# Attention stage of a fused attention and mixture-of-experts kernel: a cap on how far scores run ahead, gate products by head pair, two banks for the last outputs

## The chip, the cores and the metric

The kernel runs on one core of a Trainium2 chip. The metric is the device time of one execution in microseconds (us); lower is better. A program in the kernel file writes out the instructions of every engine in a fixed order, and each engine works through its own list in that order.

## What is computed

Four batches of eight heads, 768 tokens, head width 64, go through a local attention with block summaries; the result is the input of two mixture-of-experts layers (8 experts, 512 to 1024 to 512).

```python
k_sum = k.reshape(B, H, nb, block, D).max(axis=3)      # 24 blocks of 32 keys
v_sum = v.reshape(B, H, nb, block, D).mean(axis=3)
scores = concat(masked scale*q@k.T (|i-j| < 16), scale*q@k_sum.T + log(32))
a = softmax(scores);  attn = a @ concat(v, v_sum)
x = attn.transpose(0, 2, 1, 3).reshape(3072, 512)
logits = x @ w_gate + modality_bias[modality_id];  e = argmax(logits)
x = gate_weight * (relu(x @ w1[e]) @ w2[e])            # first expert layer
x = second expert layer: each expert takes the 384 tokens assigned to it by greedy capacity
```

## The kernel before, in words

The change lies in the attention stage and in the program that orders it. The work of the stage is cut into 48 **groups** (`QUADS`): four batches, four head pairs (`HP`), three groups per head pair. Group i has 256 query rows of two heads, and these steps:

- `scores` (L318, step "s"): eight matmuls of 64 rows into a PSUM bank with tag "s" (two such banks).
- `top_` (L330, "m"): VectorE takes the row maxima and scales them. `expo` (L335, "e"): ScalarE does four exponentials.
- `atrans` (L341, "at"): four transposes on TensorE into a bank "a" (two). `atput` (L347, "ac"): ScalarE or VectorE copies them to SBUF.
- `av` (L351, "av"): eight matmuls with the values, into the bank "o"; there is one.
- `total`, `inverse`, `put_x` (L363 to L378, "t", "r", "x"): VectorE divides by the row sums and puts the result into `xb`, which also frees the bank "o".
- `xturn` (L425, "xt"): two transposes of the result into a bank "t" (two). `xput` (L433, "xp"): a copy to SBUF, tile `xt`, three buffers.
- `gate1` (L437, "g1"): two matmuls with 8 weight columns each, which add the group's part of the gate logits in the bank `GS`. At the end of a batch come `gcopy`, `gturn`, `gput` (L449 to L461, "gc", "gt", "gp") and the batch's routing (`route1`, L505).

Once three batches are routed, `first_page` (L698) lists the first 256 tokens of the most frequent expert, gathers their rows through GpSimd's DMA queue (`gather`, L643) and issues the first four quarter loads of the expert weights (`wraw`) on SyncE's queue. `first_turn` and `first_split` ("ft", "fs") transpose and split these rows, `Quarters.high` and `low` ("hi", "lo") split the first four weight quarters into a high and a low part, all among the last groups of the attention.

**What sets the order.** `Pieces` (L753) holds every step with an order number, the engines that may take it, the steps it must follow, and the buffers it needs. `step` (L780) works with a cost model (`Clock`, L67): at each turn it takes the step that can start earliest by the model, and among those that can start then the one with the lowest order number. The step's instructions are written out at that moment, so an engine's list follows the model's times, while the chip keeps its own. The order numbers count groups: scores of group i have i, products with values i + 3, gate steps i + 5 (`LOG`), and i + 10 (`LOGT`) for the last eight groups. The rules that bound how far scores run ahead are indirect: scores of group i follow the exponentials of group i - 2, these follow the transposes of group i - 4 and so on. `av(i)` follows `put_x(i - 1)`, because there is one bank "o". The loop ends (L893) when every step is written out; the code of the first expert layer comes behind it, so on TensorE its first matmul (`s<-xhi,whi`) stands behind the last step of the attention.

Of the kernel before, what the change touches and what calls it, by code (L numbers as in the profile page):

```python
# [8 lines left out]
F32 = mybir.dt.float32  # L9
# [14 lines left out]
HP = H // 2  # L24
E = 8
# [13 lines left out]
QUADS = B * HP * 3  # L39
# [101 lines left out]
def moe_block(ctx, tc, qt, kw, vw, v, mod, wg1, mbias, w1a, w2a, wg2, w1b, w2b, out):  # L141
# [138 lines left out]
    def vsum(i):  # L280
# [9 lines left out]
        else:  # L290
            VB[0] = vb

    XB = {}
    PS, NM, EX, AT, RD = {}, {}, {}, {}, {}

# [54 lines left out]

    def av(i):  # L351
        g, c = divmod(i, 3)
        p = bank("o")
        PS["o", i] = pv = p[:, :4 * (D + 1)].rearrange("p (u c) -> p u c", u=4)
        for t in range(2):
            for h in range(2):
                for s in range(2):
                    P.matmul(pv[s * 64:(s + 1) * 64, 2 * t + h, :],
                             AT[i][:UC, 2 * t + h, s * 64:(s + 1) * 64],
                             VW[g % NV][:UC, s, h, 2 * c + t, :], start=True, stop=True)  # L360
        AT.pop(i)
# [59 lines left out]
    XS = {}  # L421
# [9 lines left out]
            P.transpose(p[:, t * 128:(t + 1) * 128], XB[b][:, 2 * c + t, hp * 128:(hp + 1) * 128], ident)  # L431

    def xput(j, e):  # L433
        XS[j] = ld.tile([128, 256], F32, name="xt", bufs=3)
        copy(e, XS[j], PS.pop(("x", j))[:, :256])

    def gate1(j):  # L437

        g, c = divmod(j, 3)
        b, hp = divmod(g, HP)  # L440
        x, o = XS.pop(j), (b % 2) * 256 + c // 2 * 128
        if hp == c == 0:
            P.matmul(GS[0][:, o:o + 256], zb, zb[:, None, :].to_broadcast([128, 2, 128]), start=True, stop=False, skip_group_check=True)
        for t in range(2):
            r0 = 32 * (2 * (c % 2) + t)
            P.matmul(GS[0][r0:r0 + E, o:o + 128], wg1s[:, hp], x[:, t * 128:(t + 1) * 128], start=False, stop=(hp == HP - 1),
                     skip_group_check=True)

    def gcopy(b, e):  # L449
        XS["g", b] = t = ld.tile([128, 256], F32, name="gst", bufs=1)  # L450
# [278 lines left out]
    EPA = 0  # L729
    GRP = -3.5  # L730
    AHEAD = 4
    LOGT = 10
    HL = 1000
    LOG = 5
    THR = -10
    BIAS = 0.3
    WARM = 6
# [15 lines left out]
    class Pieces:  # L753
# [26 lines left out]
        def step(self):  # L780
            best = {}
            for name, (order, on, fn, after, take, give, cost) in self.todo.items():
                if any(x not in self.end for x in after) or take and not self.free():
                    continue
                t, e = min((self.start(e, after, take) + (BIAS if len(on) > 1 and e == "V" else 0.0), e) for e in on)
                best.setdefault(e, []).append((t, order, name))
            if self.thread is None and self.queue and self.queue[0][1] in self.end:
                self.thread, self.want, self.ready = self.queue.pop(0)[0], "V", 0.0
            if self.thread and (self.want != "P" or self.free()):
                e = "P" if self.want == "P" else "V"  # L790
                best.setdefault(e, []).append((max(clock.at[e], self.ready), THR + self.base, None))
            lo = {e: min(x) for e, x in best.items()}
            e = min(lo, key=lambda x: lo[x])
            t = lo[e][0]
            name = min((x for x in best[e] if x[0] <= t + EPA), key=lambda x: x[1])[2]
            clock.last = 0.0
            if name is None:
                if self.want == "P":
                    self.slots.append([("thread",), None])
                was, self.want = self.want, next(self.thread, None)  # L800
                if was != "P":
                    self.give(("thread",))
                self.ready = clock.after("P" if self.want == "P" else "V")
                if self.want is None:
                    self.thread = None
                return
            order, on, fn, after, take, give, cost = self.todo.pop(name)
            self.base = order if name[0] == "s" else self.base
            if take:
                self.slots.append([name, None])  # L810
            for x in after:
                if e in "VAP" and x[0] in ("lk", "lq", "lv", "lvs", "lvb", "fv", "fi", "qs", "c"):
                    clock.at[e] = max(clock.at[e], self.end[x])
            if cost is not None:
                clock.at[e] = clock.last = max(clock.at[e], t) + cost
            if len(on) > 1:
                fn(e)
            else:
                fn()
            if give:  # L820
                self.give(give)
            self.end[name], self.by[name] = clock.last + (2.0 if e == "D" else 0.0), e
# [7 lines left out]
    for g in range(NG):  # L830
# [12 lines left out]
        for c in range(3):  # L843
            i = 3 * g + c
            pc.add(("s", i), i, "P", L_(scores, i),
                   [("kc", h, g) for h in range(2)] + [("lq", g)]
                   + [("s", i - 1), ("e", i - 2)])
            pc.add(("m", i), i + OM, "V", L_(top_, i), [("s", i), ("e", i - 3), ("m", i - 1)])
            pc.add(("e", i), i + OE, "A", L_(expo, i), [("m", i), ("e", i - 1), ("at", i - 4)])
            pc.add(("at", i), i + OAT, "P", L_(atrans, i), [("e", i), ("ac", i - 2), ("at", i - 1)])  # L850
            pc.add(("ac", i), i + OAC, "AV", L_(atput, i), [("at", i), ("ac", i - 1), ("av", i - 3)])
            pc.add(("av", i), i + OAV, "P", L_(av, i), [("ac", i), ("av", i - 1), ("x", i - 1), ("lv", g), ("vr", g)])
            pc.add(("t", i), i + OX, "V", L_(total, i), [("av", i)])
            pc.add(("r", i), i + OX, "V", L_(inverse, i), [("t", i)])
            old = 3 * HP * (b - 1) - 1
            pc.add(("x", i), i + OX, "V", L_(put_x, i), [("r", i), ("x", i - 1)] + ([("xt", old), ("sx", old)] if b > 1 else []))
            if g % HP == HP - 1:
                pc.add(("sx", i), i, "D", L_(store_x, b, c), [("x", i)], cost=1.5)
            pc.add(("xt", i), i + (LOG if i < QUADS - 8 else LOGT), "P", L_(xturn, i), [("x", i), ("xt", i - 1)], take=1)
            pc.add(("xp", i), i + OXP + (LOG if i < QUADS - 8 else LOGT), "AV", L_(xput, i), [("xt", i), ("xp", i - 1), ("g1", i - 3)], give=("xt", i))  # L860
            pc.add(("g1", i), i + (LOG if i < QUADS - 8 else LOGT), "P", L_(gate1, i), [("xp", i), ("g1", i - 1), ("lc", 0)])
        if g % HP == HP - 1:
            o = 3 * g + 2 + (LOG if g < NG - 3 else LOGT)
            pc.add(("gc", b), o + OGP, "AV", L_(gcopy, b), [("g1", 3 * g + 2)])
            pc.add(("gt", b), o + OGP, "P", L_(gturn, b), [("gc", b)], take=1)
            pc.add(("gp", b), o + OGP, "V", L_(gput, b), [("gt", b), ("bc", 0)], give=("gt", b))
    zl = qk.tile([128, NTOK // 128 * E], F32, name="zl")
# [1014 lines left out]
```

## Time and profile before

| | us |
|---|---|
| median of three runs (885.65 to 888.65) | 886.11 |
| the profiled execution: its time | 885.47 |
| its span, first to last instruction | 883.6 |
| TensorE busy (share of the span) | 800.4 (91%) |
| VectorE busy | 669.1 (76%) |
| ScalarE busy | 423.9 (48%) |
| mean granted TensorE clock | 0.958 |

In the profile, "line" is L136 for nearly everything, since one helper issues the compute instructions; the tile names tell the steps apart: `s<-kw,qt` scores, `a<-ident,ex` the transposes behind the exponentials, `o<-vw,at` products with values, `t<-ident,xb` the transposes of results, `gs<-xt,wg1s` gate products, `t<-ident,xr` the transposes of the first gathered rows, `s<-xhi,whi` the first expert matmul. An fp32 matmul leaves two records: a group has 16 records of scores, 16 of products, 4 of gate products; a transpose leaves one. A timeline row gives start and length of a run of like instructions; the next run can start before the end of the one before it, since matmuls overlap. PEclk 1.00 is 2.4 GHz and 0.50 is 1.2 GHz.

### The profile page before, as it was taken

How to read it: one execution, taken by the hardware profiler on the slowest of the kernel's cores; microseconds unless marked ns; L12 is line 12 of the kernel's file. 1: busy time of each engine (PE TensorE's matmuls, PEld its weight loads, DVE VectorE, ACT ScalarE, POOL GpSimd, SP SyncE). 2: the span in 40 equal slices, each digit the busy share in tenths (PEclk: the TensorE clock that was granted, in tenths of full speed). 3: DMA queues.
4: the chain of work that ended last, by engine and by line, in shares of the span. 5: the costliest groups of instructions: out<-in, count | busy, mean ns of one | idle time of the engine just before them, and what ended most of it. 6: DMA issues, size and time to landing. Idle time of an engine off the chain costs nothing. (4 is left out here: it accounts for less than half of the span.)

```text
span 883.6 us, 17809 instructions
## 1 busy us (share of the span) xinstructions
PE 800.4 (91%) x6457; PEld 672.1 (76%) x6457; DVE 669.1 (76%) x1908; ACT 423.9 (48%) x769; POOL 223.7 (25%) x354
## 2 busy tenths in 40 slices
PE   4888899779999999999999924999999999998997
PEld 3666667558998899999999822878786878787895
DVE  7978786659884888888888758788797979786540
ACT  4665566443566855555555512334343343333440
POOL 6453821302142233223322212011112020204011
PEclk9999989879999999999999955999999999999999
DMA  7789866455679576656665304253434353437410
GB/s 243 226 255 314 269 214 198 148 168 167 212 245 329 170 239 224 208 200 216 227 200 198 119 22 143 84 178 104 160 112 163 120 167 120 145 119 245 143 65 36
DMA packets 93093, 157.16 MB, mean 178 GB/s; under 512 B 10332, under 2 KB 53620, under 8 KB 92228
## 3 DMA queue, kind: packets, MB, share of 16 engines
q1 hardware_dynamic: 83652, 128.91, 45.6%
q0 software_dynamic: 8800, 25.96, 8.6%
q8 instruction: 53, 0.87, 0.4%
q10 hardware_dynamic: 544, 1.05, 0.4%
q14 instruction: 44, 0.36, 0.1%
HBM read 136.36 MB, written 19.53 MB: 176 GB/s over the span
## 5 line engine op out<-in xcount | busy, mean ns | idle before, releaser
L136 DVE TENSOR_TENSOR wlo<-wraw,whi 128x512 fp32r<-128x512 f32 x336 | 218.6, 685 | 21.9 <-ACT whi L136 20.3
L136 ACT ACTIVATE whi<-wraw 128x1024 fp32r<-128x1024 f32 x168 | 176.2, 1056 | 61.0 <-DMA wraw<-in_moe_w_dram 59.4
L136 PE MATMUL s<-xhi,whi 128*128 128x256 f32 (+1 forms) x640 | 197.4, 311 | 2.2 <-DVE hlo L136 1.5
L136 PE MATMUL s<-xhi,wlo 128*128 128x256 f32 (+1 forms) x640 | 196.2, 309 | 0.0
L136 PE MATMUL s<-xlo,whi 128*128 128x256 f32 (+1 forms) x640 | 189.3, 310 | 0.0
L136 PE MATMUL a<-wlo,hhi 128*128 128x512 f32 x328 | 131.4, 401 | 0.0
L136 PE MATMUL a<-whi,hhi 128*128 128x512 f32 x328 | 130.1, 397 | 0.0
L136 PE MATMUL a<-whi,hlo 128*128 128x512 f32 x328 | 129.5, 395 | 0.0
L136 PEld LDWEIGHTS s<-xhi,whi 128*128 128x128 f32 x640 | 122.6, 191 | 5.6 <-ACT xhi L136 3.0
L136 PEld LDWEIGHTS s<-xhi,wlo 128*128 128x128 f32 x640 | 122.6, 192 | 0.7
L136 ACT ACTIVATE hhi<-s 128x384 fp32r<-128x384 f32 (+1 forms) x112 | 60.0, 535 | 130.6 <-PE s L136 130.5
L136 PEld LDWEIGHTS s<-xlo,whi 128*128 128x128 f32 x640 | 119.6, 191 | 0.2
L136 DVE SCALAR_TENSOR_TENSOR hlo<-s,hhi 128x384 fp32r<-128x384 f32 (+1 forms) x112 | 68.0, 608 | 22.3 <-ACT hhi L136 22.1
L136 PEld LDWEIGHTS a<-whi,hlo 128*128 128x128 f32 x328 | 61.7, 188 | 11.9
L136 PEld LDWEIGHTS a<-whi,hhi 128*128 128x128 f32 x328 | 61.7, 188 | 11.9
L136 PEld LDWEIGHTS a<-wlo,hhi 128*128 128x128 f32 x328 | 61.7, 188 | 11.1
L136 ACT ACTIVATE ex<-s,nm 128x120 f32<-128x120 f32 x192 | 53.6, 365 | 32.8 <-DVE nm L136 28.7
L1763 POOL DMA_INDIRECT xr<-y_d,ix x24 | 26.5, 1105 | 165.5 <-DVE key L136 123.4
L136 PE MATMUL s<-kw,qt 128*64 128x120 f32 x768 | 54.6, 289 | 11.3 <-ACT kw L136 9.7
L136 ACT ACTIVATE xhi<-t 128x512 fp32r<-128x512 f32 x49 | 28.1, 596 | 73.5 <-PE t L136 73.5
L1094 POOL DMA_INDIRECT y_d<-y,six x25 | 30.5, 1219 | 112.6 <-ACT y L136 109.8
L136 PEld LDWEIGHTS s<-kw,qt 128*64 128x64 f32 x768 | 42.9, 147 | 20.9 <-ACT kw L136 11.0
(305 smaller groups left out, 1258.2 us busy)
## 6 DMA issues: line engine op xcount, KB each, us to landing
wraw<-in_moe_w_dram SPq DMA_DIRECT2D x166, 512.0 KB
kw<-in_kw_dram SPq DMA_DIRECT2D x32, 324.0 KB
vw<-in_vw_dram SPq DMA_DIRECT2D x32, 292.5 KB
vb<-in_v_dram SPq DMA_DIRECT2D x6, 1024.0 KB
qt<-in_qt_dram SPq DMA_DIRECT2D x32, 192.0 KB
x_d<-xb SPq DMA_DIRECT2D x12, 512.0 KB
hr<-in_moe_w_gate_dram SPq DMA_DIRECT2D x4, 512.0 KB
wraw<-in_moe_w_dram ACTq DMA_DIRECT2D x2, 512.0 KB
```

The costliest lines, as they stand in the source:

```text
L136: return fn(*args, **kw)
L1094: st = G.indirect_dma_start(out=dst, out_offset=bass.IndirectOffsetOnAxis(ap=six[:, c:c + 1], axis=0), in_=rows, in_offset=None)
L1763: G.indirect_dma_start(out=t, out_offset=None, in_=y_d[:NTOK], in_offset=bass.IndirectOffsetOnAxis(ap=IX[k][:, i:i + 1], axis=0))
```

## The change

1. **Cap on scores.** Scores of group i must also follow the products of group i - 4 (`LAG = 4`).
2. **Two banks at the end.** The products of groups 45 and 47 (`SPARE`) go to a bank with tag "s". Products of groups 45 to 47 follow `put_x` of the group two back, not one back.
3. **Gate products by head pair.** `gate1` is called once per head pair, behind the three `xput` of its groups, and issues the six matmuls in one run. `xt` has four buffers.
4. **Order numbers of the gate steps**: i + 4 everywhere (`LOG = 4`); `LOGT` is gone.
5. **Planner's start times**: for "hi" and "ft" the model now counts when the weight quarter or the gathered rows land (`clock.ready`).

```diff
+    SPARE = (QUADS - 3, QUADS - 1)
...
     def av(i):
         g, c = divmod(i, 3)
-        p = bank("o")
+        p = bank("s" if i in SPARE else "o")
...
-        XS[j] = ld.tile([128, 256], F32, name="xt", bufs=3)
+        XS[j] = ld.tile([128, 256], F32, name="xt", bufs=4)
...
-    def gate1(j):
-
-        g, c = divmod(j, 3)
+    def gate1(g):
+
         b, hp = divmod(g, HP)
-        x, o = XS.pop(j), (b % 2) * 256 + c // 2 * 128
-        if hp == c == 0:
+        o = b % 2 * 256
+        if hp == 0:
             P.matmul(GS[0][:, o:o + 256], zb, zb[:, None, :].to_broadcast([128, 2, 128]), start=True, stop=False, skip_group_check=True)
-        for t in range(2):
-            r0 = 32 * (2 * (c % 2) + t)
-            P.matmul(GS[0][r0:r0 + E, o:o + 128], wg1s[:, hp], x[:, t * 128:(t + 1) * 128], start=False, stop=(hp == HP - 1),
-                     skip_group_check=True)
+        for c in range(3):
+            x = XS.pop(3 * g + c)
+            for t in range(2):
+                r0, o1 = 32 * (2 * (c % 2) + t), o + c // 2 * 128
+                P.matmul(GS[0][r0:r0 + E, o1:o1 + 128], wg1s[:, hp], x[:, t * 128:(t + 1) * 128], start=False, stop=(hp == HP - 1),
+                         skip_group_check=True)
...
-    LOGT = 10
-    LOG = 5
+    LOG = 4
+    LAG = 4
...
+                x = QS[0].raw.get(name[1]) if name[0] == "hi" else XR.get(name[1]) if name[0] == "ft" else None
+                if x is not None:
+                    t = max(t, clock.ready(x, e))
...
             pc.add(("s", i), i, "P", L_(scores, i),
                    [("kc", h, g) for h in range(2)] + [("lq", g)]
-                   + [("s", i - 1), ("e", i - 2)])
+                   + [("s", i - 1), ("e", i - 2), ("av", i - LAG)])
...
-            pc.add(("av", i), i + OAV, "P", L_(av, i), [("ac", i), ("av", i - 1), ("x", i - 1), ("lv", g), ("vr", g)])
+            pc.add(("av", i), i + OAV, "P", L_(av, i), [("ac", i), ("av", i - 1), ("x", i - (2 if i in SPARE or i - 1 in SPARE else 1)), ("lv", g), ("vr", g)])
...
-            pc.add(("xp", i), i + OXP + (LOG if i < QUADS - 8 else LOGT), "AV", L_(xput, i), [("xt", i), ("xp", i - 1), ("g1", i - 3)], give=("xt", i))
-            pc.add(("g1", i), i + (LOG if i < QUADS - 8 else LOGT), "P", L_(gate1, i), [("xp", i), ("g1", i - 1), ("lc", 0)])
+            pc.add(("xp", i), i + OXP + LOG, "AV", L_(xput, i), [("xt", i), ("xp", i - 1), ("g1", (i - 4) // 3)], give=("xt", i))
+        pc.add(("g1", g), 3 * g + 2 + LOG, "P", L_(gate1, g), [("xp", 3 * g + c) for c in range(3)] + [("g1", g - 1), ("lc", 0)])
```

## Rows read from the trace of the kernel before

**Rows 1.** Page, part 2: granted TensorE clock in 40 slices of the span (tenths).
```profile
PEclk9999989879999999999999955999999999999999
```
**Rows 2.** Busy time of each engine by stretch, in us; last columns clock, DMA share, GB/s.
```profile
core 0: us, PE busy (x) PEld busy (x) DVE busy (x) ACT busy (x) POOL busy (x), PEclk, DMA share, GB/s
...
171.22:178.09 6.87, 6.87 (x57) 5.04 (x57) 3.38 (x10) 3.29 (x6) 2.69 (x11) 0.56 0.08 30
...
183.99:192.28 8.29, 6.21 (x53) 3.42 (x53) 1.53 (x6) 1.65 (x5) 0.00 (x0) 0.50 0.86 282
13.72:163.88 150.16, 133.73 (x1862) 102.07 (x1862) 117.92 (x328) 91.70 (x285) 63.20 (x114) 0.95 0.77 240
...
192.28:883.60 691.32, 643.89 (x4371) 556.01 (x4369) 524.97 (x1510) 314.05 (x451) 144.50 (x198) 0.97 0.50 162
```
**Rows 3.** The same view for tile qt: the PE count is score records, 16 a group.
```profile
27.60:50.70 23.10, 9.16 (x128) 7.18 (x128) 0.00 (x0) 0.00 (x0) 0.00 (x0) 0.94 0.77 242
...
85.10:102.20 17.10, 6.25 (x96) 4.88 (x96) 0.00 (x0) 0.00 (x0) 0.00 (x0) 1.00 0.72 242
...
0.00:50.70 50.70, 16.78 (x208) 13.32 (x208) 1.62 (x1) 1.65 (x2) 3.31 (x3) 0.97 0.79 244
0.00:102.20 102.20, 33.60 (x464) 26.58 (x464) 1.62 (x1) 1.65 (x2) 3.31 (x3) 0.97 0.82 254
0.00:131.40 131.40, 44.18 (x608) 34.81 (x608) 1.62 (x1) 1.65 (x2) 3.31 (x3) 0.95 0.81 255
0.00:163.87 163.87, 53.55 (x752) 42.13 (x752) 1.62 (x1) 1.65 (x2) 3.31 (x3) 0.96 0.76 237
```
**Rows 4.** The same for tile vw (PE, PEld, POOL): product records, 16 a group.
```profile
163.87:192.28 28.41, 6.69 (x112) 5.59 (x112) 0.00 (x0) 0.73 0.67 214
...
0.00:50.70 50.70, 6.64 (x144) 5.72 (x144) 6.41 (x18) 0.97 0.79 244
0.00:102.20 102.20, 17.26 (x368) 14.60 (x368) 19.72 (x46) 0.97 0.82 254
0.00:131.40 131.40, 22.87 (x480) 19.52 (x480) 24.33 (x56) 0.95 0.81 255
0.00:163.87 163.87, 30.47 (x656) 25.85 (x656) 31.18 (x70) 0.96 0.76 237
```
**Rows 5.** Timeline of TensorE, 135 to 143 us: start, length, what.
```profile
135.20 0.69 PE L136 MATMUL o<-vw,at 120*64 120x65 f32 x16
135.82 0.44 PE L136 MATMUL t<-ident,xb 128*128 128x128 f32 x2
136.18 1.04 PE L136 MATMUL s<-kw,qt 128*64 128x120 f32 x16
137.16 0.39 PE L136 MATMUL gs<-xt,wg1s 128*8 128x128 f32 x4
137.48 0.69 PE L136 MATMUL o<-vw,at 120*64 120x65 f32 x16
...
141.86 1.04 PE L136 MATMUL s<-kw,qt 128*64 128x120 f32 x16
142.73 0.46 PE L136 MATMUL o<-vw,at 120*64 120x65 f32 x10
```
**Rows 6.** Timeline of TensorE, 162 to 193 us; in brackets idle before and releaser.
```profile
162.90 0.69 PE L136 MATMUL o<-vw,at 120*64 120x65 f32 x16 [1.68 <-DVE mk L136]
...
171.22 1.09 PE L136 MATMUL t<-ident,xr 128*128 128x128 f32 x4 [3.78 <-DMA xr<-x_d,gix]
...
178.09 0.61 PE L136 MATMUL gs<-xt,wg1s 128*8 128x128 f32 x8
178.63 0.69 PE L136 MATMUL o<-vw,at 120*64 120x65 f32 x16
...
186.81 1.14 PE L136 MATMUL o<-vw,at 120*64 120x65 f32 x16
...
192.28 0.56 PE L136 MATMUL s<-xhi,whi 128*128 128x256 f32 x1
```
**Rows 7.** Timeline of ScalarE, 163 to 192 us.
```profile
166.03 1.12 ACT L136 ACTIVATE ex<-s,nm 128x120 f32<-128x120 f32 x4 [0.46 <-DVE nm L136]
...
179.64 0.59 ACT L136 ACTIVATE at<-a 120x512 f32<-120x512 f32 x1
```
**Rows 8.** Timeline of SyncE's queue, 150 to 206 us.
```profile
161.65 2.12 SPq L589 DMA_DIRECT2D wraw<-in_moe_w_dram  x4
177.57 6.22 SPq L592 DMA_DIRECT2D wraw<-in_moe_w_dram  x4
```

More of the change, by code (lines that the diff above doesn't have):

```diff
@@ L858, in moe_block @@
                 pc.add(("sx", i), i, "D", L_(store_x, b, c), [("x", i)], cost=1.5)
-            pc.add(("xt", i), i + (LOG if i < QUADS - 8 else LOGT), "P", L_(xturn, i), [("x", i), ("xt", i - 1)], take=1)
-            pc.add(("xp", i), i + OXP + (LOG if i < QUADS - 8 else LOGT), "AV", L_(xput, i), [("xt", i), ("xp", i - 1), ("g1", i - 3)], give=("xt", i))
-            pc.add(("g1", i), i + (LOG if i < QUADS - 8 else LOGT), "P", L_(gate1, i), [("xp", i), ("g1", i - 1), ("lc", 0)])
+            pc.add(("xt", i), i + LOG, "P", L_(xturn, i), [("x", i), ("xt", i - 1)], take=1)
+            pc.add(("xp", i), i + OXP + LOG, "AV", L_(xput, i), [("xt", i), ("xp", i - 1), ("g1", (i - 4) // 3)], give=("xt", i))
+        pc.add(("g1", g), 3 * g + 2 + LOG, "P", L_(gate1, g), [("xp", 3 * g + c) for c in range(3)] + [("g1", g - 1), ("lc", 0)])
         if g % HP == HP - 1:
-            o = 3 * g + 2 + (LOG if g < NG - 3 else LOGT)
-            pc.add(("gc", b), o + OGP, "AV", L_(gcopy, b), [("g1", 3 * g + 2)])
+            o = 3 * g + 2 + LOG
+            pc.add(("gc", b), o + OGP, "AV", L_(gcopy, b), [("g1", g)])
             pc.add(("gt", b), o + OGP, "P", L_(gturn, b), [("gc", b)], take=1)
```

## The prediction

> **What bounds the kernel now.** I read the page's clock line first [rows 1]: of 40 slices of 22 us two are at half, and the rest near full. The dip near 540 us lies in the second routing, which the change does not touch. For the attention I went from the clock to busy time by stretch [rows 2]. From 13.72 to 163.88 us TensorE is busy 133.73 of 150.16 us (89%), VectorE 117.92 (79%), ScalarE 91.70 (61%): TensorE sets the pace with some holes. From 183.99 to 192.28 us its clock is 0.50 and it is still idle for 2.08 of 8.29 us, with VectorE and ScalarE at a fifth: nothing is the bound there but a chain of single steps.
>
> The counts by tile say why that tail is long. At 163.87 us 752/16 = 47 groups of scores have run [rows 3], but only 656/16 = 41 groups of products [rows 4]. Behind it come one group of scores and 112/16 = 7 groups of products [rows 4], in 28.4 us. In the timeline [rows 6] that stretch holds a wait of 3.78 us for the first gathered rows, whose transposes stand in TensorE's list ahead of products that could have run; the clock is 0.56 in the 6.87 us behind it [rows 2]. Then the products come one at a time through the single bank "o", each with its transposes and a gate product that waits for a copy, until the first expert matmul at 192.28 us.
>
> **The change part by part.** I follow one number, the start of the first expert matmul; what lies behind it takes 691.32 us [rows 2].
>
> *Last scores, moved products.* With the cap four products are left behind the last scores instead of seven, so three run ahead of them. One costs TensorE 0.62 us for the products (135.20 to 135.82), 0.36 for the transposes (135.82 to 136.18) and 0.32 for the gate (137.16 to 137.48) [rows 5]: 1.30, so the last scores move by +3.9 us. They started at 163.88 us.
>
> *Gate products.* A pair costs 0.32 us. Eight records, two pairs in one run, cost 178.63 - 178.09 = 0.54 [rows 6], so a further pair costs 0.22 and a run of three 0.76 instead of 0.96. The pair also costs the group ahead of it: scores take 0.98 us to the start of a gate pair but 0.87 to the start of products [rows 5], 0.11 more, twice saved per run. In all 0.20 + 0.22 = 0.42 us per head pair, 6.3 us over the 15 runs ahead of the last scores. This counts where TensorE is the bound. Bounds: 0 (a wait takes it) and -6.3; TensorE is busy 89%, but VectorE's 79% is near, so I take -3.7, somewhat over half.
>
> *What the cap takes away.* The lead of scores over products was 13 - 9 = 4 at 50.70 us, 29 - 23 = 6 at 102.20, 38 - 30 = 8 at 131.40 and 47 - 41 = 6 at 163.87 [rows 3, 4]. It rose by about five groups in all, counting the part ahead of 50.70 as one. Where it rose, scores filled time in which products were late; now TensorE waits there. The price of a lost fill is at most the scores and the transposes behind them, 0.98 + 0.6 = 1.6 us, so 8 us in all; at the least nothing, where the planner merely preferred scores to products that were ready. A small gain is not excluded either. That work isn't gone: it is done later, in place of the scores that ran ahead before, and the count of work ahead of the last scores is the same but for the three products above. I take +4: the place at 162.90 us, where products waited 1.68 us for VectorE's routing burst [rows 6] although the lead was 6, says that late products are real. Queued behind such a wait are the next scores, and VectorE's maxima wait for them.
>
> *The planner's start times.* With the landing counted, the gathered rows' transposes no longer stand ahead of ready products: the 3.78 us wait goes, and so does the cold stretch behind it. The next thing late is the chain of the last group. The weight splits move the same way on ScalarE and VectorE; they lie beside the chain and can each delay one of its steps by up to an instruction. GpSimd's two gathers and SyncE's first four quarter loads (161.65 us [rows 8]) hang on the gate of the third batch, which comes somewhat earlier.
>
> *The last chain.* From the last scores at 163.88 to the end of their exponentials at 166.03 + 1.12 = 167.15 us are 3.27 us [rows 7]. Then four transposes (at most 0.7, twice the pair's 0.36), their copy 0.59 [rows 7] and two handovers, about 0.1 each: 4.8 us to the last products. The three products that are left before it fit into this time, 3 x 1.30 = 3.9, since two more banks hold them: this is what hides them. With one bank each would wait for the division of the one before. From the last products at 186.81 to the expert matmul at 192.28 are 5.47 us [rows 6], at half clock. The last run of gate products is now three pairs, 0.76 for 0.32: +0.4. In all 10.7 us, which I take; at full clock the second half shortens, by about 1.3 us (products 0.69 for 1.14, the rest in like proportion).
>
> On the clock in this chain: the trace shows 0.50 in 183.99 to 192.28, where TensorE worked in short runs with waits between [rows 2]. The Trainium skill, "TensorE: Matmul & The Clock Gate", section on a second failure mode (depth-cycling of the PSUM queue), says that short idles between groups that cycle through banks can make the clock swing between its two levels. It speaks against this change, which leaves a tail of just this kind and may add waits in the middle; by it the chain is 10.7 us as taken, and at full clock it would be 9.4.
>
> On the gate run: the trace shows pairs in one pair of column positions only. The Trainium skill, "TensorEngine Tiling (Array Packing)", Key Properties, says that different tiles can load and multiply in parallel; by that the first four products of a run would go together and a run would cost 0.54, not 0.76, another 3.3 us over 15 runs. No row here shows four at once.
>
> *Sum.* Last scores at 163.88 + 3.9 - 3.7 + 4 = 168.1; first expert matmul at 168.1 + 10.7 = 178.8 instead of 192.28: -13.5 us. Behind it the order of work is the same and I cost it at 0. What hides it: quarters five to eight were issued from 177.57 us [rows 8], and are wanted only behind the first layer of the first page. Since a planner with shifted clocks may order that part a little differently, I give it 3 us to each side. The profiled execution took 885.47 us, 883.6 of span and 1.9 around it, 0.6 under the median 886.11; -13.5 from the median gives **872.6 us**.
>
> **The rivals.** (a) *The middle gives half back.* All fills lost at the full price (+4 over what I took) and the gate runs buy nothing (+3.7): 872.6 + 7.7 = 880.3. For it: 79% on VectorE, whose bursts stop products. Against it: the stretch with a lead of 3 to 4 ran 8 groups in 23.10 us, 2.89 each, and one with a lead of 6 ran 6 in 17.10, 2.85 each [rows 3], so a short lead costs little.
>
> (b) *The cap starves TensorE, slower.* With a lead of four every hiccup of ScalarE or VectorE (late key loads, maxima, routing) reaches TensorE's list, since scores, transposes and products then all wait for the same two engines. Some 34 groups ran with a lead over 4. The rest of the sum is -17.5 without the fills, so this decides from 17.5/34 = 0.5 us per group; at 0.7 us each it is +23.8 and the time 886.1 - 17.5 + 23.8 = 892.4. Against it: the same two stretches, 2.89 against 2.85.
>
> (c) *The expert layer cannot use an earlier start.* If the first gathered rows and weight splits stay where they were, or the routing of the fourth batch, on which the weight loads of later pages hang, arrives no earlier, the gain is waited away: 886. Against it: all of them hang on attention steps that move up too.
>
> (d) *Part of the change does nothing.* If the planner still writes the last products one behind the other, each behind its copy, the two banks are idle and the chain keeps about 3 us: 875.6. This stays inside the forecast's own range.
>
> (e) *The gate runs pay more*, and the middle loses nothing: 872.6 - 2.6 - 4 = 866.
>
> **How the numbers follow.** Forecast with (d) 0.60, (a) 0.20, (e) 0.07, (c) 0.06, (b) 0.07. The unknown terms, -2.6 to +3.7, -4 to +4, -1.3 to 0, 3 each way, give about 6 us each way when they don't all fall together: 866 to 879. To leave out no more than 2 in 10 the range takes in most of (a) and (e): 863 to 882. A measurement here tells 0.3%, 2.7 us, from no change. Faster by more: 0.60 + 0.20 + 0.07 = 0.87. Within it: 0.06, slower 0.07.
>
> **What would show it.** In the changed profile: products behind the last scores are 64 records, not 112; gate products in runs of 12 records of some 0.76 us; no wait for gathered rows over 1 us; first expert matmul near 179 us and some 691 us behind it. Wrong would be: waits of products or scores on VectorE and ScalarE between 50 and 160 us that grow by over 8 us (then (a) or (b)), a first expert matmul that is early while the span behind it grows (then (c)).

## The result, and the profile after

The changed kernel takes 883.08 us (median of 20 runs, 876.52 to 889.3) against 891.00 for the kernel before in the same 20 rounds (885.65 to 898.65): a ratio of 0.9911, with an interval of 0.9887 to 0.9935. It is faster by 0.9%, about 7.9 us (5.8 to 10.1), where 13.5 were forecast. The three runs of before that stood ahead of the prediction (886.11) lie low among the 20. So the direction is right, the gain is a little over half of the forecast, and 883.08 lies 1.1 us above the range.

The head of the page after, with the clock row that answers to [rows 1]:

```profile
span 881.7 us, 17767 instructions
...
PE 794.7 (90%) x6457; PEld 667.1 (76%) x6457; DVE 667.2 (76%) x1900; ACT 429.2 (49%) x777; POOL 224.5 (25%) x354
...
PEclk9988999999999999999999955999999999999999
```

The span is 1.9 us under the 883.6 of before; but the execution profiled there took 885.47 us, less than any of the 20, so the two profiles make the gain look small. I then read the number that the prediction followed, in busy time by stretch: up to the last scores, the tail to the first expert matmul, and the rest. Columns are those of [rows 2].

```profile
13.70:177.40 163.70, 135.74 (x1950) 102.04 (x1950) 120.96 (x337) 100.10 (x298) 69.41 (x128) 0.94 0.75 235
...
177.45:190.15 12.70, 9.22 (x134) 6.58 (x133) 9.42 (x26) 8.98 (x23) 0.35 (x2) 1.00 0.70 220
...
190.15:881.70 691.55, 646.92 (x4371) 557.76 (x4370) 524.61 (x1510) 314.31 (x451) 144.59 (x198) 0.96 0.50 164
```

The rest takes 691.55 us, as before [rows 2]. The tail from the last scores to the first expert matmul is 12.70 us, where it was 28.4. But the last scores start at 177.45 us, 13.6 later than before, where +4.2 was forecast. So the tail paid and the middle, the stretch up to the last scores, gave most of it back: idle time of TensorE ahead of the last scores grew from 16.43 us (150.16 - 133.73, [rows 2]) to 27.96 (163.70 - 135.74).

What it waits for shows in the view of TensorE's waits (engine, tile, what it waited for: us in total, times, longest). First the kernel before, from 14 to 164 us:

```profile
PE s L136 <- ACT kw L136: 9.7, 2, 9.5
PE o L136 <- DVE xb L136: 5.0, 5, 1.9
```

and the changed kernel, from 14 to 178 us:

```profile
PE t L136 <- DVE xb L136: 16.5, 12, 5.5
PE s L136 <- ACT kw L136: 9.7, 2, 9.5
PE a L136 <- ACT ex L136: 6.1, 5, 2.9
```

The wait of 9.7 us for the first keys is common to both. New is the first line: the transposes of results `t` wait 16.5 us for the division `xb` (`put_x`). In the kernel before it is the products `o` that wait for `xb`, and for 5.0 us only. TensorE's timeline of the changed kernel shows where it comes from (start, length, what; in brackets idle before and releaser):

```profile
43.30 0.44 PE L136 MATMUL t<-ident,xb 128*128 128x128 f32 x2 [2.20 <-DVE xb L136]
43.66 0.69 PE L136 MATMUL o<-vw,at 120*64 120x65 f32 x16
...
45.10 0.61 PE L136 MATMUL gs<-xt,wg1s 128*8 128x128 f32 x12
45.64 0.44 PE L136 MATMUL t<-ident,xb 128*128 128x128 f32 x2
...
49.75 1.04 PE L136 MATMUL s<-kw,qt 128*64 128x120 f32 x16
56.27 0.69 PE L136 MATMUL t<-ident,xb 128*128 128x128 f32 x2 [5.48 <-DVE xb L136]
56.75 1.06 PE L136 MATMUL a<-ident,ex 128*120 128x128 f32 x4
57.74 1.03 PE L136 MATMUL gs<-xt,wg1s 128*8 128x128 f32 x12
58.70 1.13 PE L136 MATMUL o<-vw,at 120*64 120x65 f32 x16
...
64.11 0.44 PE L136 MATMUL t<-ident,xb 128*128 128x128 f32 x2
64.47 0.69 PE L136 MATMUL o<-vw,at 120*64 120x65 f32 x16
65.09 0.65 PE L136 MATMUL a<-ident,ex 128*120 128x128 f32 x4
65.67 1.04 PE L136 MATMUL s<-kw,qt 128*64 128x120 f32 x16
66.65 0.44 PE L136 MATMUL t<-ident,xb 128*128 128x128 f32 x2
```

The transposes `t` of the newest result now mostly stand directly ahead of the next products `o`; in [rows 5] they stand behind them. When VectorE is late with `xb`, all of TensorE stops at the transposes. At 56.27 VectorE was late because of a key load, as its timeline shows:

```profile
52.41 0.95 DVE L136 TENSOR_REDUCE kmx<-kw 128x24 f32<-128x768 f32 x1 [4.84 <-DMA kw<-in_kw_dram]
...
55.79 0.42 DVE L136 TENSOR_TENSOR xb<-o,rd 128x256 f32<-128x256 f32 x1
```

VectorE stood 4.84 us for keys of a later group with the division `xb` behind it in its list. After this wait the runs are longer for some us (1.03 for the gate run at 57.74, and 0.61 for that at 45.10): the granted clock is 0.63 from 56 to 61 us and 1.00 from 61 to 66, so a long wait is paid a second time.

### The profile page after: what moved, and what is told of

The parts are those of the page before. It is cut to its first block, busy times and chain, and to the rows that moved or that the text cites. A ratio compares the mean times of both kernels' runs of the same rounds, so it can differ in the third digit from the quotient of the medians.

```text
span 881.7 us, 17767 instructions
## 1 busy us (share of the span) xinstructions
PE 794.7 (90%) x6457; PEld 667.1 (76%) x6457; DVE 667.2 (76%) x1900; ACT 429.2 (49%) x777; POOL 224.5 (25%) x354
## 5 line engine op out<-in xcount | busy, mean ns | idle before, releaser
L136 DVE TENSOR_TENSOR wlo<-wraw,whi 128x512 fp32r<-128x512 f32 x336 | 218.4, 684 | 23.9 <-ACT whi L136 22.6
L136 PE MATMUL s<-xlo,whi 128*128 128x256 f32 (+1 forms) x640 | 189.6, 310 | 0.2 <-DVE xlo L136 0.2
L136 PEld LDWEIGHTS a<-whi,hlo 128*128 128x128 f32 x328 | 62.4, 190 | 12.3
L136 PE MATMUL s<-kw,qt 128*64 128x120 f32 x768 | 52.7, 282 | 10.2 <-ACT kw L136 9.7
L136 DVE TENSOR_TENSOR xlo<-t,xhi 128x512 fp32r<-128x512 f32 x49 | 32.6, 687 | 31.8 <-ACT xhi L136 31.8
```

The costliest lines, as they stand in the source:

```text
L136: return fn(*args, **kw)
```

## The experiments

One profiled execution scatters: three traces of the kernel before and four of the changed one give the spread below. All numbers but the ratios are us. "Last s" is the start of the last group of scores, "first e" that of the first expert matmul, "tail" the difference, "rest" the span behind it; each is from one trace. Times are medians of all executions; ratios are to the kernel before in the same rounds, with intervals.

| run | last s | first e | tail | rest | time | ratio |
|---|---|---|---|---|---|---|
| before, 3 traces | 162.9 to 163.9 | 191.5 to 192.7 | 28.4 to 29.6 | 691.3 to 696.4 | | 1 |
| changed, 4 traces | 175.2 to 177.5 | 188.9 to 190.4 | 12.7 to 14.0 | 690.1 to 694.4 | 883.08 | 0.9911 (0.9887 to 0.9935) |
| e1 no cap | 171.2 | 188.0 | 16.9 | 698.6 | 880.64 | 0.9896 (0.9857 to 0.9936) |
| e2 cap alone | 177.0 | 189.4 | 12.3 | 689.8 | 885.04 | 0.9941 (0.9907 to 0.9974) |
| e3 landing alone | 162.6 | 185.2 | 22.6 | 702.4 | 884.85 | 0.9934 (0.9904 to 0.9963) |
| e4 gate by group | 177.4 | 189.1 | 11.7 | 694.0 | 880.13 | 0.9893 (0.9858 to 0.9927) |
| e9 `LOG` 5 | 165.5 | 177.2 | 11.7 | 695.8 | 877.80 | 0.9878 (0.9834 to 0.9922) |
| e14 the same again | 167.8 | 179.5 | 11.7 | 692.8 | 876.49 | 0.9852 (0.9806 to 0.9899) |
| e13 transposes behind | 167.0 | 178.7 | 11.7 | 696.7 | 878.16 | 0.9868 (0.9817 to 0.9919) |
| e15 changed, beside e13, e14 | 176.5 | 190.4 | 14.0 | 690.5 | 884.80 | 0.9939 (0.9910 to 0.9969) |
| e10 no cap, `LOG` 5 | 155.8 | 180.3 | 24.6 | 693.8 | 876.19 | 0.9850 (0.9811 to 0.9888) |
| e11 late cap, `LOG` 5 | 171.7 | 182.5 | 10.7 | 690.5 | 874.89 | 0.9833 (0.9796 to 0.9870) |
| e16 the same again | 170.7 | 181.4 | 10.7 | 688.1 | 871.74 | 0.9780 (0.9726 to 0.9835) |
| e12 before, late cap | 173.8 | 186.6 | 12.8 | 696.4 | 880.51 | 0.9899 (0.9866 to 0.9932) |
| e17 e9, keys later | 167.3 | 179.1 | 11.8 | 691.0 | 877.03 | 0.9863 (0.9808 to 0.9917) |
| e18 e11, keys later | 166.7 | 178.5 | 11.8 | 693.0 | 874.19 | 0.9814 (0.9765 to 0.9862) |

**One part at a time.** My first theory was that the cap takes away fills that were worth more than I had priced.

e1, the changed kernel without the cap:

```diff
-                   + [("s", i - 1), ("e", i - 2), ("av", i - LAG)])
+                   + [("s", i - 1), ("e", i - 2)])
```

> The changed kernel without the cap (scores need not follow the products of group i - 4); all else as changed. Theory 1 (the cap takes away scores that would fill TensorE while VectorE waits for late key loads): last scores start near 166 us instead of 177.5, six or seven product groups behind them instead of four, first expert matmul near 184 to 187 us, time 3 to 6 us below the changed kernel, waits of TensorE on xb and ex between 14 and 165 us at most half of the 22.6 us of the changed kernel. Theory 2 (a late key load stops VectorE's list, on which scores hang as much as products, so the lead covers nothing): the same waits stay within 5 us of 22.6, the tail is longer by the three products, first expert matmul at or behind 190 us, time 0 to 5 us above the changed kernel.

e2, the kernel before with the cap (`LAG = 4`) alone:

```diff
-                   + [("s", i - 1), ("e", i - 2)])
+                   + [("s", i - 1), ("e", i - 2), ("av", i - LAG)])
```

> The kernel before with the cap of four alone (one bank for outputs, gate products by group, old order numbers, old start times). Theory 1: the middle loses some 9 us of fill, the tail gains three groups of 2.8 us each, 8.4 us; time within 3 us of the kernel before. Theory 2: the cap costs nothing in the middle beyond the three products that move (4 us) and the tail gains 8.4 us; time 3 to 6 us below the kernel before.

e3, the kernel before with the landing times alone:

```diff
+                x = QS[0].raw.get(name[1]) if name[0] == "hi" else XR.get(name[1]) if name[0] == "ft" else None
+                if x is not None:
+                    t = max(t, clock.ready(x, e))
```

> The kernel before with only the planner's start times for hi and ft counting the landing. Both theories: the wait for the gathered rows (3.78 us in the kernel before) goes, and with it the half clock behind it; if that is the larger part of the gain, the time is 4 to 8 us below the kernel before; if the tail is a chain of single products anyway, less than 3 us below.

e4, the changed kernel with gate products by group, as before (`LOG` still 4):

```diff
...
-            pc.add(("xp", i), i + OXP + LOG, "AV", L_(xput, i), [("xt", i), ("xp", i - 1), ("g1", (i - 4) // 3)], give=("xt", i))
-        pc.add(("g1", g), 3 * g + 2 + LOG, "P", L_(gate1, g), [("xp", 3 * g + c) for c in range(3)] + [("g1", g - 1), ("lc", 0)])
+            pc.add(("xp", i), i + OXP + LOG, "AV", L_(xput, i), [("xt", i), ("xp", i - 1), ("g1", i - 4)], give=("xt", i))
+            pc.add(("g1", i), i + LOG, "P", L_(gate1, i), [("xp", i), ("g1", i - 1), ("lc", 0)])
...
```

> The changed kernel with gate products group by group again (two matmuls each, 48 runs instead of 16). By the price of 0.42 us per head pair: 6 us above the changed kernel if TensorE is the bound everywhere, 2 to 4 us if waits take half of it. A rival: the longer run delays what stands behind it and the time is within 1 us.

Cap and landing times each gain some 0.6% alone. The landing times bring the first expert matmul from 192.2 (mean of three) to 185.2, but e3's one trace has a long rest, 702.4. The cap alone brings it to 189.4. Without the cap, e1 lies between what the theories expected: the last scores still come at 171.2, so much of the lost time is not the cap's. And without the gate runs e4 is no slower. Its stretch up to the last scores is the row to read against the changed kernel's 135.74 of 163.70:

```profile
13.70:177.40 163.70, 142.79 (x1951) 104.80 (x1953) 123.28 (x336) 101.59 (x301) 69.11 (x128) 0.94 0.77 235
```

TensorE is busy 142.8 us here and 135.7 to 137.4 in the four traces of the changed kernel, so the gate runs do save it 6.3 us on the mean (136.5). But idle time is 20.9 us here and 25.4 to 28.0 there (26.1 on the mean): 5.2 us of the 6.3 came back as waits.

**Scatter.** Two more traces each of the two kernels, unedited (e5, e7 before; e6, e8 changed):

> The kernel before, unchanged, for a second trace. If the part behind the first expert matmul (691.3 us in its first trace) and the time of the last scores vary from execution to execution, its span lies several us above 883.6, near the median of 890, and the difference sits in waits for key loads before 164 us or in the first four pages of expert weights. If these are fixed by the order of the program, the trace repeats within 2 us.

> The changed kernel, unchanged, for a second trace. If executions vary, the waits for key loads on VectorE (11.5 us, the longest 4.8) come out otherwise, and the last scores start elsewhere than 177.2 us; if the order of the program fixes them, they repeat within 2 us, and so does the part behind the first expert matmul (691.6 us).

> The kernel before, unchanged, for a third trace; the same as said for the second.

> The changed kernel, unchanged, for a third trace; the same as said for the second.

Their times were 890.86, 885.76, 887.11 and 880.76. The last scores and the first expert matmul repeat within 2.3 us, the rest within 5.1; so the first two carry the argument, and one trace's rest proves nothing.

**The order numbers.** What was left was an edit that the prediction had passed over: part 4 of the change. With `LOG = 4` the transposes of group i have the order number i + 4. The products of group i + 1 have i + 1 + 3, the same. The planner takes the lowest number among the steps that can start, and of equal ones that which was entered first: the transposes. (Both become ready by the same event, since products of group i + 1, like the transposes of group i, follow `put_x(i)`.) In the written-out list of TensorE, transposes stand directly ahead of products 41 times and directly behind them twice; in the kernel before it is once and 37 times. e9 sets `LOG` back to 5 and leaves all the rest; e10 also drops the cap (the edit of e1); e11 keeps the cap for the last groups only:

```diff
-    LOG = 4
+    LOG = 5
...
-                   + [("s", i - 1), ("e", i - 2), ("av", i - LAG)])
+                   + [("s", i - 1), ("e", i - 2)] + ([("av", i - LAG)] if i >= 36 else []))
```

> The changed kernel with the gate steps' order numbers at i + 5 again. If the early order numbers (transposes of results ahead of the next products and scores) cost part of the middle, the last scores start 4 us or more before 176 us and the first expert matmul lies near 185; if the cap alone costs it, both stay within 1.5 us of the changed kernel's 176.1 and 189.4 (means of three traces).

> The changed kernel without the cap and with order numbers i + 5: planner's start times, two banks and gate runs are left. If cap and order numbers are what costs the middle, the last scores start at or before 163 us (kernel before: 163.3, mean of three traces) with eight products behind them, and the first expert matmul lies near 183 to 186. If the gate runs cost it, the last scores stay near 170 as without the cap alone.

> Order numbers i + 5 and the cap only for scores of group 36 and later, all else as changed. Theory: the cap costs where key and value loads come late, between 27 and 85 us, and pays only at the end. Then the stretch up to 110 us is as in the kernel before, the last scores start near 170, the tail is 12 to 13 us, the first expert matmul lies near 182 to 184, and the time is 5 us or more below the changed kernel if the part behind it stays at 692. Rival: a lead once built must be paid back as products before the last scores, wherever the cap sits; first expert matmul near 189.

With one number changed (3 pairs ahead, 39 behind) the last scores come at 165.5 and the first expert matmul at 177.2, 12.4 us earlier than the changed kernel's mean of 189.6. It is the same without the cap: this one number brings e1's first expert matmul from 188.0 to 180.3 in e10. e13 breaks the tie in another way, by a tenth for the transposes alone (4 ahead, 39 behind), and e14 and e15 repeat e9 and the changed kernel beside it:

```diff
-            pc.add(("xt", i), i + LOG, "P", L_(xturn, i), [("x", i), ("xt", i - 1)], take=1)
+            pc.add(("xt", i), i + LOG + 0.1, "P", L_(xturn, i), [("x", i), ("xt", i - 1)], take=1)
```

> The changed kernel with one order number moved by a tenth: the transposes of results at i + 4.1 instead of i + 4; copies and gate products stay at LOG = 4. It breaks the tie in which the transposes of group i and the products of group i + 1, both ready when put_x(i) is done, have the same number and the transposes are written first; in TensorE's list the pair transposes-products then stands the other way round some 39 times. Theory: this tie is all that LOG = 4 costs; last scores near 165 us, first expert matmul near 177, time within 3 us of the kernel with LOG = 5 (877.8). Rival: the early copies on ScalarE and VectorE cost it; then all stays near the changed kernel, 176, 189.4 and 883.

> The changed kernel with LOG = 5, once more, on the same chip and beside the changed kernel. First expert matmul 177 us again if the order fixes it. If the start is given back behind, the part from there to the end is 695 us or more again and the time is 4 to 6 us below the changed kernel; if the 695.8 of the first trace was chance, the part is near 692 and the time 10 to 12 us below.

> The changed kernel on the same chip: first expert matmul near 189.4 us, 692 us behind it, time near 883.

e13 and e14 give the same: first expert matmul at 178.7 and 179.5, times 878.16 and 876.49 against 884.80 (e14's interval stands clear of e15's, e13's just overlaps it). So the tie costs about 11 us at the first expert matmul and 6.6 to 8.3 us in time, and one order number does it: e13 moves that of the transposes and no other. The lists of the other engines shift a little with it (up to the last scores VectorE has 350 instructions in e13 and 337 in the changed kernel, ScalarE 287 and 298), which no run parts from the swap itself. e14's stretch up to the last scores shows how:

```profile
13.70:167.80 154.10, 132.13 (x1950) 105.48 (x1950) 122.24 (x351) 92.35 (x286) 68.36 (x127) 0.94 0.83 250
```

These are 1950 records of TensorE, as many as in the changed kernel, so the same work. The three traces with the tie broken (e9, e13, e14) are busy 131.8 us on the mean and idle 21.3; the four of the changed kernel are busy 136.5 and idle 26.1. Of the 9.5 us about half is idle, and about half is TensorE itself being busy longer with the same work. The waits of TensorE are in the same view as above, from 14 to 168 us of e14; the last line is VectorE's wait for products, from 13 to 190 us:

```profile
PE o L136 <- DVE xb L136: 7.7, 9, 4.2
...
PE t L136 <- DVE xb L136: 0.9, 1, 0.9
...
DVE rd L136 <- PE o L136: 5.6, 7, 1.6
```

The same line in the changed kernel:

```profile
DVE rd L136 <- PE o L136: 11.1, 18, 1.3
```

The transposes wait 0.9 us instead of 16.5. Part of that is only a change of name, as the products now stand first and wait for the same `xb`: both together wait 8.6 us here (5.5 and 8.9 in e9 and e13), where the four traces of the changed kernel have 12.9 to 16.5. What the order changes is when the products start. VectorE's next division hangs on them, while only the gate steps hang on the transposes. With the transposes first VectorE waits 10.6 to 12.1 us for products in the four traces, with the tie broken 5.0 to 6.5. That the ring from products to division and on to the next products became longer is read from these waits; no run parts it from the rest. The busier half is seen in one undisturbed group of e14's timeline, to be read against 64.11 to 66.65 above:

```profile
63.76 0.69 PE L136 MATMUL o<-vw,at 120*64 120x65 f32 x16 [1.17 <-DVE xb L136]
64.37 0.44 PE L136 MATMUL t<-ident,xb 128*128 128x128 f32 x2
64.65 0.60 PE L136 MATMUL a<-ident,ex 128*120 128x128 f32 x4
65.18 1.04 PE L136 MATMUL s<-kw,qt 128*64 128x120 f32 x16
66.05 0.64 PE L136 MATMUL o<-vw,at 120*64 120x65 f32 x16
```

A group takes 66.05 - 63.76 = 2.29 us from products to products in this order and 66.65 - 64.11 = 2.54 in the other. Scores take 0.87 to the start of products and 0.98 to the start of transposes; and the two kinds of transposes, one behind the other, take 0.28 and 0.53, where apart they take 0.36 and 0.58. The four runs stand together in the dear order in only some 14 of the changed kernel's 48 groups, which makes 3.5 us of the 4.7; part of the busy time is at the lower clock behind long waits. I have not parted these, and no row shows why one order is dearer.

e12 puts the late cap on the kernel before, with landing times and spare banks but gates by group, `LOG` 5 and `LOGT` 10; e16 repeats e11:

```diff
+    SPARE = (QUADS - 3, QUADS - 1)
...
-        p = bank("o")
+        p = bank("s" if i in SPARE else "o")
...
+                x = QS[0].raw.get(name[1]) if name[0] == "hi" else XR.get(name[1]) if name[0] == "ft" else None
+                if x is not None:
+                    t = max(t, clock.ready(x, e))
...
-                   + [("s", i - 1), ("e", i - 2)])
+                   + [("s", i - 1), ("e", i - 2)] + ([("av", i - 4)] if i >= 36 else []))
...
```

> The kernel before with the planner's start times, the two banks for the last outputs and the cap only from group 36; gate products by group, old order numbers. Up to 130 us its order is that of the kernel before. Theory: last scores near 168 to 170, tail 12 to 15 us (late gate steps of the last eight groups lengthen it), first expert matmul near 182 to 184. Against the run before it this shows what gate runs bring: 2 to 6 us if they bring something.

> The cap from group 36 with order numbers i + 5, once more: if the cap costs in the middle and pays at the end, 2 to 4 us below the kernel with LOG = 5 and the cap everywhere; if the place of the cap does not matter, within 2 us of it.

e12 was to show what gate runs bring once the tie is gone. Against e11, in the same rounds, its first expert matmul comes 4.1 us later (186.6 and 182.5) and its time is 5.6 us longer (880.51 and 874.89; the intervals of the ratios overlap by a hair). Up to the last scores it is busy 140.3 us where e11 and e16 are busy 135.6 and 134.8, and idle 19.8 where they are idle 22.4 and 22.2. So about half of the saved busy time counts there. Since e12 also keeps `LOGT` at 10, not all of the difference need be the gate runs'.

**What the cap is worth once the tie is gone.** e10, without any cap, takes 876.19, and e9 and e14, with the cap everywhere, 877.80 and 876.49: the cap shortens the tail from 24.6 to 11.7 us and delays the last scores by 11, so it buys nothing that these runs can tell. Kept for the last twelve groups it has the shortest tail, 10.7, and the lowest times, 874.89 and 871.74, though the intervals of e11 and e16 overlap with those of e9 and e14 in the same rounds. Its first expert matmul lies 2 to 5 us behind theirs, so a lower time would have to come from the rest (690.5 and 688.1), which scatters by 5 us between traces; why it should is open. Both stand clear of the changed kernel's interval in the table: late cap with `LOG` 5 beats both kernels, by 1.7% to 2.2% against before.

**Key loads.** VectorE's wait for keys (`kmx`) was 6.7 to 11.5 us in the four traces of the changed kernel and 3.0 to 6.3 in the three of before, so a rival was that late loads set the middle. e17 and e18, both with `LOG` 5, let the planner reckon that keys land 3 us later, so that other steps are written ahead of what waits for them:

```diff
+    KL = 3.0
...
-                t = max(t, self.end[x] + (-2.0 if e == self.by[x] == "D" else clock.lag(self.by[x], e)))
+                t = max(t, self.end[x] + (-2.0 if e == self.by[x] == "D" else clock.lag(self.by[x], e)) + (KL if x[0] == "lk" and e != "D" else 0.0))
...
-                    clock.at[e] = max(clock.at[e], self.end[x])
+                    clock.at[e] = max(clock.at[e], self.end[x] + (KL if x[0] == "lk" else 0.0))
```

> LOG = 5 with the cap everywhere, and the planner told that key loads land 3 us later than it assumed, so that the maxima over key blocks stand later in VectorE's list. If VectorE's list, stopped by a late key load, is what the short lead cannot cover, waits of VectorE for key loads fall from 4 to 7 us to under 3, waits of TensorE on xb before 164 us by 3 us or more, and the first expert matmul lies at 174 to 176 us instead of 178.4 (mean of two traces). Rival: the loads bound the stage by themselves (transfers are busy 82 to 91% between 27 and 85 us); TensorE then waits for the same time elsewhere, and the matmul stays at 177 to 180.

> The same for the kernel with the cap from group 36: by the first view its first expert matmul moves from 182 to 178 to 180 us and the time from 873 to about 870; by the rival nothing moves by more than 2 us.

VectorE's wait for keys fell to 1.1 us in e17 (4.4 and 7.4 in e9 and e14) and to 1.7 in e18, but e17's first expert matmul (179.1) and time (877.03) are those of e9 and e14, and TensorE is idle 20.9 us ahead of the last scores, as there (20.2 and 22.0). So the wait moved to other places, as the rival on record had it; that the loads themselves bound the stage is not shown by it. With the tie in place this was not tried. e18 moved its first expert matmul to 178.5 and gained no time that can be told (874.19).

## Why the prediction was right and wrong

**The step that failed: the order numbers of the gate steps were costed at nothing, because they were not costed at all.** The prediction goes through the cap, the banks, the gate runs and the landing times; that `LOG` 4 also moves the transposes of results, and moves them to a tie with the products, is in the diff and in none of its terms. The tie put 16.5 us of waits for `xb` on the transposes and cost 11 us at the first expert matmul. With it broken and all else as in the change, the forecast's path comes out nearly number for number, and the ratios, 0.985 to 0.988, come near the 0.985 of the forecast:

| | forecast | tie broken (e9, e14, e13) | changed kernel |
|---|---|---|---|
| last scores | 168.1 | 165.5, 167.8, 167.0 | 175.2 to 177.5 |
| tail | 10.7 | 11.7 | 12.7 to 14.0 |
| first expert matmul | 178.8 | 177.2, 179.5, 178.7 | 188.9 to 190.4 |

That the sum agrees so closely is partly luck, since its terms for the gate runs and the chain were each off, as said below.

**The moved products** were right in kind and count: four groups of products stand behind the last scores, not seven (in the changed kernel's timeline at 178.78, 180.48, 183.40 and 184.38 us).

**The last chain** was 1.0 us short with the tie broken, 2.0 in this trace, and wrong in its working. This is the changed kernel's tail:

```profile
177.45 1.04 PE L136 MATMUL s<-kw,qt 128*64 128x120 f32 x16
178.42 0.44 PE L136 MATMUL t<-ident,xb 128*128 128x128 f32 x2
178.78 0.69 PE L136 MATMUL o<-vw,at 120*64 120x65 f32 x16
180.48 0.78 PE L136 MATMUL s<-vw,at 120*64 120x65 f32 x16 [1.01 <-issue]
181.19 1.09 PE L136 MATMUL t<-ident,xr 128*128 128x128 f32 x8
182.11 1.04 PE L136 MATMUL a<-ident,ex 128*120 128x128 f32 x8
183.40 0.69 PE L136 MATMUL o<-vw,at 120*64 120x65 f32 x16 [0.25 <-ACT at L136]
184.38 0.69 PE L136 MATMUL s<-vw,at 120*64 120x65 f32 x16 [0.29 <-ACT at L136]
...
189.95 0.44 PE L136 MATMUL t<-ident,gst 128*128 128x128 f32 x2 [0.48 <-ACT gst L136]
190.15 0.37 PE L136 MATMUL s<-xhi,whi 128*128 128x256 f32 x1
```

No wait for gathered rows over 1 us is left, as forecast: `t<-ident,xr` runs at once. The clock did not fall: the tail's row above has 1.00 where 0.50 was taken over from [rows 2], and three of the four products there take 0.69 us, not the 1.14 of [rows 6]. Of the three other traces of the changed kernel one has 1.00 too, two have 0.88 and 0.84. The Trainium skill, "TensorE: Matmul & The Clock Gate", section on a second failure mode, led me to expect a swing between the two levels in such a tail; by it 10.7 us, at full clock 9.4. This trace shows full clock and 12.7 us, so no swing in it. From the last scores to the last products it takes 184.38 - 177.45 = 6.93 us for the 4.8 of the sum, and from there 5.77 for 5.87, though the latter was reckoned at half clock. What I had left unpriced are the weight splits among the chain's steps. ScalarE's timeline:

```profile
179.26 1.12 ACT L136 ACTIVATE ex<-s,nm 128x120 f32<-128x120 f32 x4
180.23 1.09 ACT L136 ACTIVATE whi<-wraw 128x1024 fp32r<-128x1024 f32 x1
181.18 1.15 ACT L136 ACTIVATE ex<-s,nm 128x120 f32<-128x120 f32 x4
182.75 0.60 ACT L136 ACTIVATE at<-a 120x512 f32<-120x512 f32 x1 [0.42 <-PE a L136]
183.25 0.59 ACT L136 ACTIVATE xhi<-t 128x512 fp32r<-128x512 f32 x1
183.72 0.60 ACT L136 ACTIVATE at<-a 120x512 f32<-120x512 f32 x1
```

A split `whi` of 1.09 us stands between the last two exponentials and `xhi` between the last two copies: beside the chain by the prediction, in it by the trace.

Nor are the two banks what hides the three products, as the prediction has it. e2 has one bank, with the cap alone, and its tail is no longer, 12.3 us:

```profile
168.47 1.09 PE L136 MATMUL t<-ident,xr 128*128 128x128 f32 x4 [5.02 <-DMA xr<-x_d,gix]
...
177.03 0.99 PE L136 MATMUL s<-kw,qt 128*64 128x120 f32 x16
...
182.16 0.78 PE L136 MATMUL o<-vw,at 120*64 120x65 f32 x16 [0.68 <-DVE xb L136]
...
185.65 0.69 PE L136 MATMUL o<-vw,at 120*64 120x65 f32 x16 [0.33 <-DVE xb L136]
...
189.37 0.37 PE L136 MATMUL s<-xhi,whi 128*128 128x256 f32 x1
```

Its products do wait for the divisions ahead of them, but for under 1 us each, so what the banks add is not shown. The first row shows what the landing times are for: without them the wait for gathered rows stays, 5.02 us, and with the cap it stands ahead of the last scores. In no trace with the landing times, e3's among them, is it left.

**The gate runs** cost less than the sum took: twelve records take 45.64 - 45.10 = 0.54 us, as much as eight do in [rows 6], where the sum took 0.76. By the rule of the Trainium skill, "TensorEngine Tiling (Array Packing)", Key Properties, the prediction had 0.54 as the other value, and this row agrees with it. In all, though, e4 against the changed kernel shows 6.3 us of busy time saved, the very 6.3 that went with 0.76, and not the 9.6 that 0.54 would add up to; where the other 3.3 went is open. How much of it counts depends on the tie. With the tie in place 5.2 us come back as idle and no gain in time can be told, as in rival (a)'s second half, "the gate runs buy nothing". Without it, in e11 and e16 against e12, about half counts, as the sum took it.

**The cap** was to cost 4 us of lost fills. Alone (e2) it seems to cost more: the last scores go from 163.3 (mean of three) to 177.0, and idle time ahead of them from 16.5 to 25.3, or 8.8 us. But 5.02 us of that is the wait for gathered rows that stands in the tail of the kernel before; 3.8 are left. In the changed kernel the cap costs 3.7 (22.4 us idle in e1 without it, 26.1 with it). Both bear out the 4 us. With the tie broken it is 0.8 (20.5 in e10, 21.3 in e9, e13 and e14), though there as in e1 a kernel without the cap leaves more products to the tail, so these differences are rough.

**The rivals.** (a), with 880.3 for half given back, was nearest in time, and its mark (waits in the middle that grow by over 8 us) was there; but its reason was only part of it: with the tie broken TensorE's idle time ahead of the last scores falls from 26.1 to 21.3 us, where before has 16.5, so the order made about half of the growth. (b) did not happen. (c), the expert layer that cannot use an early start, may hold in part: the rest averages 695.1 us in e9, e13 and e14 against 691.6 in the changed kernel, so some 3 us of 11 may be given back. Traces of one kernel differ by up to 5 there, and e16 and e17 have a short rest (688.1 and 691.0) with an early start, so this stays open. (d) and (e): the two banks are used, as `s<-vw,at` at 180.48 and 184.38 shows, though e2's short tail does not need them; the shorter gate run of (e) is real, without its gain.

**The median.** The forecast was made against 886.11; 20 rounds put the kernel before at 891.0. Part of the miss in absolute time is due to that alone: by ratio the forecast was 0.985, and 0.9911 was measured, which from 886.11 would give 878.2, inside the range. The 5.6 us that the gain lacks are a little less than the 6.6 to 8.3 that the tie costs.

## What to carry to other kernels

When a program orders the work by priority numbers, list every step whose number a change moves, and look for ties: which of two equal steps goes first is part of the change. Where one event releases two steps of an engine whose list is worked through in order, the one that another engine waits for belongs first; here the products, behind which VectorE's next division stands. The other order in 41 groups cost 11 us at the first expert matmul. And read idle and busy time of the same count of records side by side, as a saving in busy time that comes back as idle is no saving.

## What the runs showed of the hardware

Two things stand in rows here. The order of short matmul runs changes TensorE's own busy time: the same four runs of a group take 2.29 us in e14 and 2.54 in the changed kernel, without any wait within them, at a granted clock of 1.00 in both (one group each). And the six small gate products, on four column positions, take 0.54 us in one run, 0.09 each, where a pair alone takes 0.32 [rows 5].
